# Fused attention, expert layer and MLP on one core: small VectorE steps of the attention stage rewritten, constants loaded later, one copy fewer per key-value half, a new order

## The chip, the cores and the metric

The kernel runs on one core of a Trainium2 chip. The metric is the time of one execution in microseconds (us); lower is better. A core has five engines with their own instruction streams: PE (TensorE, matrix products into PSUM), DVE (VectorE), ACT (ScalarE), POOL (GpSimd) and SP (SyncE, which here issues most of the DMA transfers). SBUF is the working memory, PSUM holds the matrix products in eight banks of 2 KB per partition. An engine works its own instructions off in the order in which they were written; semaphores hold an instruction until what it needs is done.

## The reference

Three stages, one after the other:

```python
q_s, k_s = (q * scale, k * scale)              # q, k, v: 4 batches, 8 heads, 576 tokens, 64 wide
def phi(x):                                    # omega: 128 features x 64
    h = einsum('bhsd,md->bhsm', x, omega) - sum(x * x, -1, keepdims=True) / 2
    return exp(h - max(h, -1, keepdims=True)) / sqrt(m)
q_p, k_p = (phi(q_s), phi(k_s))
kv = einsum('bhsm,bhsd->bhmd', k_p, v); z = sum(k_p, axis=2)
num = einsum('bhsm,bhmd->bhsd', q_p, kv)
den = einsum('bhsm,bhm->bhs', q_p, z)[..., None] + 1e-06
x = num / den                                  # as 2304 tokens x 512
# expert layer: each token goes to the expert with the largest logit (8 experts)
logits = x @ w_gate; expert_idx = argmax(logits, 1); probs = softmax(logits)
out[mask_e] = probs[e] * (maximum(xe @ w1[e], 0.0) @ w2[e])
# MLP: h = out @ w_in (512 -> 2048); g = h, 0 or (h + 1)**2 / 4; result g @ w_out
```

## The kernel before

The attention stage, where nearly the whole change lies, works in units. A unit is half of a block of q or k: four pairs of heads for 256 tokens (two tokens per partition), or a small block that holds the last 64 tokens of two batches. There are 36 units. In each, PE turns the data (`turn`, L640, four 128x128 products with the identity), ACT copies the result out of PSUM (`copy`, L645), PE projects it on omega into two PSUM banks (`project`, L652), DVE takes the row maxima of each bank (`top`, L657), forms the bias of the exponential from maximum and norm (`bias`, L663 and L664), and ACT takes the exponential, four instructions a bank (`exps`, L668). The norms come from the raw block: ACT (for k) or POOL (for q) squares it, POOL adds halves twice (`tree`, L603), and DVE sums the last 16 columns (`total`, L615), once for each of 20 blocks.

When all key units of half the heads of a batch are there, `kv_tasks` sums keys times values over five blocks (L694). ACT copies the result twice: once (`copy1`, L698, tile kvc) as input of a transpose on PE (`turn`, L706), once (`copy2`, L701) into kvz, where the queries read it. The transposed copy goes through the gate's weights (`gates`, L714), so that numerator, denominator and eight logits per head come from one product. There are 8 such halves. `c_tasks` (18 tiles of 128 tokens) turns the query features (L752), multiplies them with kvz (L769), copies the result out (L772, tile nx), and then runs small DVE steps: denominator (`den`), reciprocal (`rec`), logits times reciprocal (`logits`, L785, tile lg), sum over the heads.

`r_tasks` (9 pairs of tiles) is the routing: largest logit (`top`, L825), differences (`shift`, L828, tile rd), a one-hot row (`first`, `first2`, `hot`, L832 to L838, tile ohall), a running count of tokens per expert (`run`, L841, tile rsb), the softmax gate (`gate1` to `gate3`, L852 to L859), the rank of each token in its expert (`count` on PE, `mine`, `mine2`, L884 to L893), and a one-hot row of 384 columns by that rank (`one_b`, L905, tile ob), which PE turns into the list of tokens per expert. POOL scales the output rows (L869, tile xr) and SP stores them. After the last routing a fixed table is worked out on DVE, POOL gathers the first rows, and the expert layer starts with L1215. From there PE is kept full to the end.

The order is not written by hand. `Plan.add` collects tasks with an engine, a cost in ns, a rank, what they come after, and the buffers that they take and use; `Plan.run` picks one task after the other, the earliest start first and among near ones the lowest rank, and gives out buffers from rings, among them the eight PSUM banks (ring "ps"). A bank is given back when its last user is through. The table `NUDGES` holds one number for each task, which shifts its rank.

Of the kernel before, what the change touches and what calls it, by code (L numbers as in the profile page):

```python
# [8 lines left out]
F32 = mybir.dt.float32  # L9
# [27 lines left out]
C_ID, C_TRI, C_IOTA, C_C8, C_WS, C_THR, C_TOK, C_END = 0, 128, 256, 640, 648, 656, 672, 708  # L37
# [172 lines left out]
def kernel(  # L210
# [29 lines left out]
    cs = cp.tile([P, C_END], F32, name="cs")  # L240
    nc.sync.dma_start(out=cs[:, 0:P], in_=consts[:, 0:P])
    ident = cs[:, C_ID:C_ID + P]
# [4 lines left out]
    rsb = cp.tile([P, NTILE + 1, E], BF16, name="rsb")  # L247
    nc.vector.memset(rsb[:, 0, :], 0.0)
    ohall = cp.tile([P, NTILE, E], BF16, name="ohall")
# [229 lines left out]
    with ExitStack() as actx:  # L479
# [4 lines left out]
        def ring(n, shape, name, dtype=F32, pool=ac):  # L484
# [11 lines left out]
            "kvc": ring(1, [P, 4, HD], "kvc"),  # L496
# [43 lines left out]
        def omega_tasks():  # L540
            pb = buf("ps")

            def load():
                for i in range(2):
                    nc.sync.dma_start(out=om2[:, i * HD:(i + 1) * HD], in_=omega)
                nc.sync.dma_start(out=cs[:, P:C_END], in_=consts[:, P:C_END])
# [1195 lines left out]
```

## Time and profile before

| | |
|---|---|
| median of three runs | 783.35 us (782.76 to 785.56) |
| the profiled execution | 784.22 us, of which the span of the instructions is 782.4 us |
| busy share of the span | PE 95%, DVE 67%, ACT 56%, POOL 48% |
| busy time 0 to 20 us | PE 11.72 us, ACT 11.15 us, DVE 7.50 us |
| busy time 180 to 200 us | PE 20.00 us |

The shares over the whole span say little about the attention stage, which fills the first 157 us or so: there four engines are busy at once, and the windows tell which is the fullest. "Busy" counts an instruction from its start to its end, and instructions of one engine overlap at their ends, so that a full PE row is not a PE at its peak. In the rows below an idle time in square brackets names what ended it.

### The profile page before, as it was taken

To read this page: it belongs to the slowest core of one execution; us is meant where nothing else is said; L and a number is where in the kernel's file an instruction comes from. 1 tells how busy PE (TensorE), PEld (TensorE's weight loads), DVE (VectorE), ACT (ScalarE), POOL (GpSimd) and SP (SyncE) were. 2 spreads that over 40 slices of the span, in tenths; PEclk is the share of its full clock that TensorE was granted. 3 is DMA by queue.
4 is the path that set the end of the run, shared out by engine and by line. 5 is a ranking of instruction groups with operands and counts; after the bars stand their busy time and mean duration, and the time that the engine had idled before them with its cause. 6 is when DMAs were issued, how large, how long until landed. Compare 5 with 4: busy or idle time off the path is not lost. (4 is left out here: it accounts for less than half of the span.)

```text
span 782.4 us, 16983 instructions
## 1 busy us (share of the span) xinstructions
PE 746.1 (95%) x6428; PEld 684.1 (87%) x6428; DVE 525.3 (67%) x1075; ACT 439.0 (56%) x1069; POOL 377.5 (48%) x429
## 2 busy tenths in 40 slices
PE   5889999689999999999999999899999999999997
PEld 4778889569999999999998878788998899889985
DVE  3669998964875675665576776776556756575553
ACT  5999989633422222222367766676567665763341
POOL 4738673555556645533737776323343143333212
PEclk9999999899999999999999999999999999999999
DMA  9978411246556766555546778897697986977822
GB/s 221 212 166 230 146 57 30 98 137 202 178 193 196 227 195 197 181 186 162 157 127 261 274 275 289 293 377 221 205 368 174 340 297 162 349 214 299 314 104 85
DMA packets 94236, 164.25 MB, mean 210 GB/s; under 512 B 28528, under 2 KB 61424, under 8 KB 94144
## 3 DMA queue, kind: packets, MB, share of 16 engines
q1 hardware_dynamic: 79680, 94.96, 38.5%
q0 software_dynamic: 14112, 67.44, 26.7%
q8 instruction: 53, 0.87, 0.5%
q10 hardware_dynamic: 352, 0.66, 0.3%
q14 instruction: 39, 0.32, 0.1%
HBM read 122.93 MB, written 40.11 MB: 208 GB/s over the span
## 5 line engine op out<-in xcount | busy, mean ns | idle before, releaser
L1418 PE MATMUL po<-wh,g 128*128 128x512 f32 x288 | 113.9, 395 | 0.9 <-ACT st L1424 0.9
L1420 PE MATMUL po<-wh,g 128*128 128x512 f32 x288 | 113.8, 395 | 0.0
L1419 PE MATMUL po<-wl,g 128*128 128x512 f32 x288 | 113.6, 394 | 0.0
L349 POOL TENSOR_TENSOR wl<-wz,wh 128x256 fp32r<-128x256 f32 (+1 forms) x43 | 40.4, 946 | 96.7 <-ACT wh L363 92.7
L668 ACT ACTIVATE pp<-ps,bi 128x128 f32<-128x128 f32 x288 | 85.5, 487 | 2.6 <-DVE bi L664 2.6
L327 POOL TENSOR_SCALAR wh<-wra 128x1024 fp32r<-128x1024 f32 x43 | 52.1, 1215 | 56.0 <-DMA wra<-in_moe_w_dram 39.3
L1233 PE MATMUL py<-hh,wh 128*128 128x288 f32 (+6 forms) x256 | 77.5, 303 | 0.0
L1215 PE MATMUL ph<-xh,wh 128*128 128x288 f32 (+6 forms) x256 | 76.6, 299 | 0.5 <-ACT xh L1174 0.4
L1216 PE MATMUL ph<-xl,wh 128*128 128x288 f32 (+6 forms) x256 | 76.6, 299 | 0.1
L1217 PE MATMUL ph<-xh,wl 128*128 128x288 f32 (+6 forms) x256 | 76.5, 299 | 0.0
L1235 PE MATMUL py<-hh,wl 128*128 128x288 f32 (+6 forms) x256 | 76.4, 299 | 0.0
L1234 PE MATMUL py<-hl,wh 128*128 128x288 f32 (+6 forms) x256 | 76.3, 298 | 0.0
L1380 DVE TENSOR_TENSOR g<-cl,g 128x384 fp32r<-128x384 f32 x78 | 47.0, 603 | 38.9 <-ACT g L1376 37.9
L1220 ACT ACTIVATE hh<-ph 128x288 fp32r<-128x288 f32 (+6 forms) x64 | 26.8, 418 | 70.0 <-PE ph L1217 67.5
L1420 PEld LDWEIGHTS po<-wh,g 128*128 128x128 f32 x288 | 54.2, 188 | 13.1 <-DVE g L1380 0.4
L1418 PEld LDWEIGHTS po<-wh,g 128*128 128x128 f32 x288 | 54.2, 188 | 12.9 <-ACT st L1424 1.6
L1419 PEld LDWEIGHTS po<-wl,g 128*128 128x128 f32 x288 | 54.3, 188 | 11.4
L1376 ACT ACTIVATE g<-cl 128x384 fp32r<-128x384 f32 x78 | 40.6, 520 | 40.4 <-DVE cl L1375 39.2
L1221 DVE SCALAR_TENSOR_TENSOR hl<-ph,hh 128x288 fp32r<-128x288 f32 (+6 forms) x64 | 29.3, 462 | 48.9 <-ACT hh L1220 48.8
L439 DVE TENSOR_TENSOR wl<-wra,wh 128x1024 fp32r<-128x1024 f32 x43 | 58.9, 1371 | 4.7 <-POOL wh L327 4.7
L657 DVE TENSOR_REDUCE nsq<-ps 128x4 f32<-128x512 f32 x72 | 47.4, 684 | 18.4 <-PE ps L652 18.2
L1238 ACT ACTIVATE yT<-py 128x288 f32<-128x288 f32 (+7 forms) x32 | 13.4, 418 | 82.5 <-PE py L1235 79.6
(223 smaller groups left out, 2166.5 us busy)
## 6 DMA issues: line engine op xcount, KB each, us to landing
yS<-yd POOLq DMA_DIRECT2D x32, 768.0 KB, 12.7
wra<-in_moe_w_dram SPq DMA_DIRECT2D x43, 512.0 KB, 4.2
ys<-yd POOLq DMA_DIRECT2D x25, 768.0 KB, 12.4
wraw<-in_moe_w_dram SPq DMA_DIRECT2D x20, 512.0 KB, 3.9
yd<-tt SPq DMA_DIRECT2D x24, 384.0 KB, 2.4
yd<-ys SPq DMA_DIRECT2D x9, 768.0 KB, 5.2
wra<-in_moe_w_in_dram SPq DMA_DIRECT2D x12, 512.0 KB, 5.5
wra<-in_moe_w_out_dram SPq DMA_DIRECT2D x11, 512.0 KB, 7.2
```

Of the source, the lines that this page charges most:

```text
L327: nc.gpsimd.tensor_scalar(out=hi, in0=t, scalar1=1.0, scalar2=1.0, op0=ALU.mult, op1=ALU.mult)
L439: nc.vector.tensor_sub(lo, t, hi.bitcast(F32))
L668: act.activation(at(ppb)[:, 2 * j + i, :], at(pjb[i])[:, j, :], AF.Exp, bias=r["bi"][:, j, i:i + 1])
L1215: nc.tensor.matmul(ph, lhsT=wh[:, d, c], rhs=xh, start=(d == 0), stop=False)
L1216: nc.tensor.matmul(ph, lhsT=wh[:, d, c], rhs=xl, start=False, stop=False)
L1217: nc.tensor.matmul(ph, lhsT=wl[:, d, c], rhs=xh, start=False, stop=(d == 3))
L1233: nc.tensor.matmul(py, lhsT=wh[:, a, c], rhs=hh, start=(f == 0), stop=False)
L1234: nc.tensor.matmul(py, lhsT=wh[:, a, c], rhs=hl, start=False, stop=False)
L1235: nc.tensor.matmul(py, lhsT=wl[:, a, c], rhs=hh, start=False, stop=(f == 7))
L1418: nc.tensor.matmul(po, lhsT=gh[:, c], rhs=wh, start=(f == 0), stop=False)
L1419: nc.tensor.matmul(po, lhsT=gh[:, c], rhs=wl, start=False, stop=False)
L1420: nc.tensor.matmul(po, lhsT=gl[:, c], rhs=wh, start=False, stop=(f == 3))
```

## The change

1. **Two SBUF inputs avoided.** The result of `rec` is written into the PSUM bank of the second numerator, the small tiles mx, d, mm and ga of the routing into the bank that the rank's count uses. So logits, shift, first, hot and gate2 read one operand from PSUM and one from SBUF. The running count becomes a sum over a tile `seen` that holds counts and one-hot rows side by side. `mine2` sums a second time, into PSUM, and `one_b` compares with that, by a tensor_tensor in place of a tensor_scalar. In the last pair d and mm alone lie in PSUM.
2. **Bias in one sum.** The maximum is taken negated, `total` writes half the bias twice (a second, small sum), and one sum over three numbers per row gives the bias, separately for each of the two banks. The exponential of the first bank no longer waits for the second maximum.
3. **Constants.** The identity has a tile of its own; the other constants (580 columns) are loaded by a task of rank 0 instead of together with omega.
4. **Key-value copy.** `copy1` and its tile are gone. `turn` takes kvz as the stationary operand of four real products with the identity, in place of two transposes.
5. **Costs and order.** A few costs in the plan are changed, buffers are taken earlier, and `NUDGES` is a new table.

```diff
 NUDGES = (
-    -8, 0, 25, -32, -23, 7, 39, 44, 36, -21, 30, 41, 44, -2, -37, -10, 2, 21, 43, -6, 4, -11, 31, -1, -16, -8, 19,
...
+    2, -4, -40, -16, 43, -44, 37, -6, 17, -2, -26, 9, -18, 36, -44, -2, -29, -37, 32, -32, -8, -18, 33, 26, -23,
...
             def load():
                 for i in range(2):
                     nc.sync.dma_start(out=om2[:, i * HD:(i + 1) * HD], in_=omega)
-                nc.sync.dma_start(out=cs[:, P:C_END], in_=consts[:, P:C_END])
+
+            def load_cs():
+                nc.sync.dma_start(out=cs, in_=consts[:, 0:C_ID])
...
-            x = add("SP", 1300, load, -7.5)
-            add("DVE", 130, tri, 1, after=[x])
+            x = add("SP", 1300, load_cs, 0)
+            add("DVE", 130, tri, 8, after=[x])
+            x = add("SP", 100, load, -7.5)
...
             def total():
-                dve.reduce_sum(norms()[:, 0:n, 0], at(sb)[:, 0:n, 0:16], axis=AX, negate=True)
+                m = norms()[:, 0:n]
+                dve.reduce_sum(m[:, :, 0], at(sb)[:, 0:n, 0:16], axis=AX, negate=True)
+                dve.reduce_sum(m[:, :, 1], m[:, :, 0:1], axis=AX, negate=True)
...
-            def bias():
-                r["bi"] = ap.tile([P, 4, 2], F32, name="bi", tag="bi", bufs=6)
-                m = o["norms"]()[:, 8 * hf:8 * hf + 8, :]
-                dve.reduce_sum(m[:, :, 2], m[:, :, 0:2], axis=AX, negate=True)
-                dve.reduce_sum(r["bi"].rearrange("p j i -> p (j i)"), m[:, :, 0:3:2], axis=AX)
+                dve.reduce_max(m[:, i, :], at(pjb[i]), axis=AX, negate=True)
+
+            def bias(i):
...
+                m = o["norms"]()[:, 8 * hf:8 * hf + 8, :].rearrange("p (j i) x -> p i j x", i=2)
+                dve.reduce_sum(r["bi"][:, :, i], m[:, i], axis=AX)
...
-            def copy1():
-                act.activation(at(kcb), at(kvb)[:, :, 0:HD], AF.Copy)
-
...
             def turn():
                 for c in range(2):
-                    nc.tensor.transpose(at(p1)[:, c, :],
-                                        at(kcb)[:, 2 * c:2 * c + 2, :].rearrange("p h d -> p (h d)"), ident)
+                    for i, w in enumerate(HALVES):
+                        nc.tensor.matmul(at(p1)[w, c, :], lhsT=kz[:, 4 * hf + 2 * c + i, 0:HD], rhs=ident,
+                                         start=True, stop=True)
...
-                    r["rden"] = ap.tile([P, H, 1], F32, name="rden", tag="rden", bufs=2)
+                    r["rden"] = at(nmb[1])[:, 0, 96:96 + H].rearrange("p (h o) -> p h o", o=1)
...
+            inner = ("d", "mm") if last else ("mx", "d", "mm", "ga")
...
             def run(j):
-                dve.tensor_add(rsb[:, t0 + j + 1, :], rsb[:, t0 + j, :], oh[:, j, :])
+                with nc.allow_low_precision("counts of at most 18"):
+                    dve.reduce_sum(rsb[:, t0 + j + 1, :], seen[:, t0 + j].rearrange("p i e -> p e i"), axis=AX)
...
             def mine2():
                 dve.reduce_sum(rk, r["pr"], axis=AX)
+                dve.reduce_sum(at(pb)[:, 2, 0:n], r["pr"], axis=AX)
...
-                dve.tensor_scalar(out=r["ob", j], in0=cs[:, C_IOTA:C_IOTA + NB * P], scalar1=rk[:, j:j + 1],
-                                  scalar2=None, op0=ALU.is_equal)
+                dve.tensor_tensor(out=r["ob", j], in0=cs[:, C_IOTA:C_IOTA + NB * P],
+                                  in1=at(pb)[:, 2, j:j + 1].to_broadcast([P, NB * P]), op=ALU.is_equal)
...
-            m = x = add("DVE", 85, top, fast if last else rank, after=[c["end"] for c in cs_])
+            m = x = add("DVE", 85, top, fast if last else rank, after=[c["end"] for c in cs_], take=[pb], use=[pb])
```

How the order moves, at three places. In each name the number behind the underscore is the buffer.

The start on SP, the engine that issues the loads (cs are the constants, om is omega, blk the blocks of q and k), before:

```order
L241 DMA cs<-in_consts_dram 128x128
L590 DMA blk_142<-in_k_dram 128x8x128
L545 DMA om_206<-in_omega_dram 128x64 x2
L546 DMA cs<-in_consts_dram 128x580
L586 DMA blk_143<-in_k_dram 64x8x64 x2
L590 DMA blk_144<-in_k_dram 128x8x128
L590 DMA blk_145<-in_k_dram 128x8x128
L590 DMA blk_146<-in_q_dram 128x8x128
L590 DMA blk_147<-in_k_dram 128x8x128
```

and after:

```order
L244 DMA ident<-in_consts_dram 128x128
L594 DMA blk_142<-in_k_dram 128x8x128
L546 DMA om_205<-in_omega_dram 128x64 x2
L590 DMA blk_143<-in_k_dram 64x8x64 x2
L594 DMA blk_144<-in_k_dram 128x8x128
L594 DMA blk_145<-in_k_dram 128x8x128
L594 DMA blk_146<-in_q_dram 128x8x128
L549 DMA cs<-in_consts_dram 128x580
L594 DMA blk_147<-in_q_dram 128x8x128
```

The 580 columns of constants go from the fourth place to behind the fourth block; the blocks before them keep their order.

The first key-value halves on ACT (kvc and kvz are the two copies, kvt the transposed one, pp the exponentials, th the turned units), before:

```order
L701 ACTIVATE kvz_185<-ps_138 128x4x65
L668 ACTIVATE pp_161<-ps_139,bi 128x128 x4
L698 ACTIVATE kvc_178<-ps_134 128x256
L701 ACTIVATE kvz_185<-ps_134 128x4x65
L645 ACTIVATE th_151<-ps_136 128x512
L668 ACTIVATE pp_160<-ps_135,bi 128x128 x4
L710 ACTIVATE kvt_179<-ps_139 128x256
L698 ACTIVATE kvc_178<-ps_138 128x256
```

and after:

```order
L703 ACTIVATE kvz_184<-ps_134 128x4x65
L674 ACTIVATE pp_162<-ps_136,bi 128x128 x4
L703 ACTIVATE kvz_184<-ps_140 128x4x65
L713 ACTIVATE kvt_178<-ps_137 128x256
L674 ACTIVATE pp_161<-ps_138,bi 128x128 x4
L758 ACTIVATE qt_166<-ps_139 128x512
L758 ACTIVATE qt_167<-ps_136 128x512
L674 ACTIVATE pp_163<-ps_135,bi 128x128 x4
```

The two kvc copies are gone, and the first turned queries (qt) stand among the exponentials here.

The last routing on DVE (the tiles are those named above; blk are the last two output tiles), before:

```order
L905 TENSOR_SCALAR ob<-cs,rank 128x384
L855 SCALAR_TENSOR_TENSOR dall<-rga,dall 128x16
L893 TENSOR_REDUCE rank<-rpr 128x2
L835 TENSOR_REDUCE rmm<-req 128x2
L859 RECIPROCAL dall<-dall 128x16
L838 TENSOR_TENSOR ohall<-req,rmm 128x16
L869 TENSOR_TENSOR blk_143<-nx_173,dall 128x512
L841 TENSOR_TENSOR rsb<-rsb,ohall 128x8
L905 TENSOR_SCALAR ob<-cs,rank 128x384
L869 TENSOR_TENSOR blk_146<-nx_170,dall 128x256
L841 TENSOR_TENSOR rsb<-rsb,ohall 128x8
```

and after:

```order
L867 SCALAR_TENSOR_TENSOR dall<-rga,dall 128x16
L846 TENSOR_REDUCE ps_134<-req 128x2
L901 TENSOR_TENSOR rpr<-ps_138,seen 128x16
L871 RECIPROCAL dall<-dall 128x16
L849 TENSOR_TENSOR seen<-req,ps_134 128x2x8
L905 TENSOR_REDUCE rank<-rpr 128x2
L906 TENSOR_REDUCE ps_138<-rpr 128x2
L881 TENSOR_TENSOR blk_148<-nx_172,dall 128x512
L853 TENSOR_REDUCE seen<-seen 128x8
L918 TENSOR_TENSOR ob<-cs,ps_138 128x384
L853 TENSOR_REDUCE seen<-seen 128x8
L881 TENSOR_TENSOR blk_142<-nx_174,dall 128x256
```

The second sum (ps<-rpr) is new in the chain, one-hot row and count read no second SBUF operand, and gate and scaling of the last tiles stay as they were.

## Rows read from the trace of the kernel before

**Rows 1.** Busy time by stretch; us of the stretch, then each engine (instructions)

```profile
14.00:60.00 46.00, 39.84 (x924) 34.89 (x923) 29.21 (x82) 44.24 (x142) 25.05 (x25) 1.00 0.87 189
60.00:110.00 50.00, 46.13 (x959) 40.65 (x960) 48.02 (x156) 45.81 (x151) 37.79 (x48) 0.97 0.58 167
110.00:140.00 30.00, 30.00 (x708) 27.91 (x705) 26.19 (x97) 29.45 (x102) 13.73 (x24) 1.00 0.08 23
147.00:157.00 10.00, 2.97 (x60) 2.30 (x60) 9.32 (x54) 2.79 (x11) 6.49 (x15) 0.61 0.44 155
```

**Rows 2.** Waits of ACT, 14 to 147 us; total us, times, longest

```profile
ACT pp L668 <- DVE bi L664: 2.1, 4, 0.7
```

**Rows 3.** Groups of DVE by shape, 60 to 110 us; busy us, mean ns, idle before

```profile
L905 DVE TENSOR_SCALAR ob<-cs,rank 128x384 bf16<-128x384 f32 x6 | 4.0, 691 | 0.0
L841 DVE TENSOR_TENSOR rsb<-rsb,ohall 128x8 bf16<-128x8 bf16 x8 | 3.5, 443 | 0.0
L785 DVE TENSOR_TENSOR lg<-nx,rden 128x64 f32<-128x64 f32 x6 | 3.2, 544 | 0.0
L838 DVE TENSOR_TENSOR ohall<-req,rmm 128x16 bf16<-128x16 f32 x4 | 2.3, 566 | 0.0
```

**Rows 4.** The same lines over 0 to 160 us; duration in ns, min/median/max

```profile
L905 DVE TENSOR_SCALAR ob<-cs,rank x18: 365/416/1470, 64.6 to 155.3; 128x384 bf16<-128x384 f32 x18
L841 DVE TENSOR_TENSOR rsb<-rsb,ohall x18: 145/157/1884, 63.4 to 154.2; 128x8 bf16<-128x8 bf16 x18
L785 DVE TENSOR_TENSOR lg<-nx,rden x18: 213/224/1124, 56.4 to 149.4; 128x64 f32<-128x64 f32 x18
L838 DVE TENSOR_TENSOR ohall<-req,rmm x9: 121/174/1011, 62.2 to 152.1; 128x16 bf16<-128x16 f32 x9
```

**Rows 5.** Timeline about 94 to 100 us; start us, duration us

```profile
93.94 1.89 POOL L598 TENSOR_TENSOR sqt<-blk 128x1024 f32<-128x1024 f32 x1
93.97 1.88 DVE L841 TENSOR_TENSOR rsb<-rsb,ohall 128x8 bf16<-128x8 bf16 x1
...
96.19 0.16 DVE L663 TENSOR_REDUCE nsq<-nsq 128x8 f32<-128x16 f32 x1
96.39 0.17 DVE L664 TENSOR_REDUCE bi<-nsq 128x8 f32<-128x16 f32 x1
...
99.48 0.40 ACT L698 ACTIVATE kvc<-ps 128x256 f32<-128x256 f32 x1
99.74 1.17 ACT L668 ACTIVATE pp<-ps,bi 128x128 f32<-128x128 f32 x4
```

**Rows 6.** Groups of DVE by shape, 147 to 166 us

```profile
L869 DVE TENSOR_TENSOR blk<-nx,dall 128x512 f32<-128x512 f32 x1 | 0.7, 679 | 0.0
...
L889 DVE TENSOR_TENSOR rpr<-ps,ohall 128x16 f32<-128x16 f32 x3 | 0.4, 148 | 0.0
...
L869 DVE TENSOR_TENSOR blk<-nx,dall 128x256 f32<-128x256 f32 x1 | 0.4, 414 | 0.0
```

**Rows 7.** Timeline of PE alone, 126 to 136 us

```profile
129.71 2.04 PE L652 MATMUL ps<-oms,th 64*64 64x128 f32 x64
...
133.65 0.42 PE L706 MATMUL ps<-cs,kvc 128*128 128x128 f32 x2
```

**Rows 8.** Timeline of the start

```profile
2.73 0.43 SPq L546 DMA_DIRECT2D cs<-in_consts_dram  x1
...
9.04 0.63 ACT L596 ACTIVATE sqt<-blk 128x512 f32<-128x512 f32 x1 [1.80 <-DMA blk<-in_k_dram]
```

**Rows 9.** Timeline of the last routings, from 135.86 us

```profile
135.86 0.16 DVE L825 TENSOR_REDUCE rmx<-lall 128x2 f32<-128x16 f32 x1
...
144.04 0.42 DVE L905 TENSOR_SCALAR ob<-cs,rank 128x384 bf16<-128x384 f32 x1
...
146.37 1.00 DVE L841 TENSOR_TENSOR rsb<-rsb,ohall 128x8 bf16<-128x8 bf16 x1
...
152.12 0.76 DVE L838 TENSOR_TENSOR ohall<-req,rmm 128x16 bf16<-128x16 f32 x1
```

More of the change, by code (lines that the diff above doesn't have):

```diff
@@ L35 @@
 SQ = -1.0 / 16.0
-C_ID, C_TRI, C_IOTA, C_C8, C_WS, C_THR, C_TOK, C_END = 0, 128, 256, 640, 648, 656, 672, 708
+C_TRI, C_IOTA, C_C8, C_WS, C_THR, C_TOK, C_ID, C_END = 0, 128, 512, 520, 528, 544, 580, 708
 NUDGES = (
[40 rows of a table removed]
[42 rows of a table added]
 )
@@ L237 @@
     yd = [[dram.tile([P, 4 * G], F32, name=f"yd{p}{i}") for i in range(7)] for p in range(NT // G // 2)]
-    cs = cp.tile([P, C_END], F32, name="cs")
-    nc.sync.dma_start(out=cs[:, 0:P], in_=consts[:, 0:P])
-    ident = cs[:, C_ID:C_ID + P]
+    cs = cp.tile([P, C_ID], F32, name="cs")
+    ident = cp.tile([P, P], F32, name="ident")
+    nc.sync.dma_start(out=ident, in_=consts[:, C_ID:C_END])
     trib = cp.tile([P, P], BF16, name="trib")
@@ L246 @@
     lall = cp.tile([P, NTILE, E], F32, name="lall")
-    rsb = cp.tile([P, NTILE + 1, E], BF16, name="rsb")
+    seen = cp.tile([P, NTILE + 1, 2, E], BF16, name="seen")
+    rsb, ohall = seen[:, :, 0], seen[:, 0:NTILE, 1]
     nc.vector.memset(rsb[:, 0, :], 0.0)
-    ohall = cp.tile([P, NTILE, E], BF16, name="ohall")
     rank_ = cp.tile([P, NTILE], F32, name="rank")
@@ L495 @@
             "xr": ring(3, [P, H, HD], "xr"),
-            "kvc": ring(1, [P, 4, HD], "kvc"),
             "kvt": ring(1, [P, 2, P], "kvt"),
@@ L626, in block_tasks @@
                         use=[o["buf"]])
-            t = add("POOL", 50 + 2400 * f, tree, rank - 0.4, after=[t], use=[sb])
-            o["sq"] = add("DVE", 100 + 260 * f, total, rank - 0.3, after=[t], use=[sb])
+            t = add("POOL", 2250 * f, tree, rank - 0.4, after=[t], use=[sb])
+            o["sq"] = add("DVE", 360 if small else 460, total, rank - 0.3, after=[t], use=[sb])
             return o
@@ L655, in top @@
             def top(i):
[L656 to L664 removed]
+                m = o["norms"]()[:, 8 * hf:8 * hf + 8, 2].rearrange("p (j i) -> p i j", i=2)
+                dve.reduce_max(m[:, i, :], at(pjb[i]), axis=AX, negate=True)
+            def bias(i):
+                if "bi" not in r:
+                    r["bi"] = ap.tile([P, 4, 2], F32, name="bi", tag="bi", bufs=6)
+                m = o["norms"]()[:, 8 * hf:8 * hf + 8, :].rearrange("p (j i) x -> p i j x", i=2)
+                dve.reduce_sum(r["bi"][:, :, i], m[:, i], axis=AX)
             def exps(i):
@@ L675, in unit_tasks @@
                         take=[] if c else pjb, use=[thb] + pjb, mode="quarters")
-            ends, tb, t = [], x, x
+            ends, tb, tp = [], x, x
             for i in range(2):
-                t = add("DVE", 600, lambda i=i: top(i), rank + 4.5, after=[t], use=[pjb[i]])
-            t = add("DVE", 290, bias, rank + 1, after=[t, o["sq"]])
-            for i in range(2):
+                tb = add("DVE", 600, lambda i=i: top(i), rank + 4.5, after=[tb], use=[pjb[i]])
+                t = add("DVE", 100, lambda i=i: bias(i), rank + 1, after=[tb, o["sq"]])
                 ends.append(add("ACT", 1003, lambda i=i: exps(i), rank + 2, after=[t] + ends[0:1],
                                 take=[ppb] if i == 0 else [], use=[pjb[i]]))
-            return {"done": ends, "buf": ppb, "ta": ta, "tb": tb}
+            return {"done": ends, "buf": ppb, "ta": ta, "tb": tp}
         def kv_tasks(b, hf, a, st, rank, vload):
             kz = kvz[b][:, 0:H * HZ].rearrange("p (h c) -> p h c", c=HZ)
-            kvb, kcb, ktb, p1, p2 = [buf(n) for n in ("ps", "kvc", "kvt", "ps", "ps")]
+            kvb, ktb, p1, p2 = [buf(n) for n in ("ps", "kvt", "ps", "ps")]
             def head(h):
@@ L729, in kv_tasks @@
                 heads.append(t)
-            c1 = add("ACT", 265, copy1, rank + 1, after=[t], take=[kcb], use=[kvb])
             c2 = add("ACT", 270, copy2, rank + 1, after=[t], use=[kvb])
-            t = add("PE", 216, turn, rank + 1.2, after=[c1], take=[p1], use=[kcb], mode="whole")
+            t = add("PE", 450, turn, rank + 1.2, after=[c2], take=[p1], mode="halves")
             t = add("ACT", 265, copy3, rank + 1.2, after=[t], take=[ktb], use=[p1])
@@ L803, in c_tasks @@
                         use=[nmb[hf]])
-            for fn, cost in ((den, 98), (rec, 113), (logits, 290), (logits_sum, 190)):
-                x = add("DVE", cost, fn, rank - (20 if t >= NTILE - 2 else 3.4), after=[x])
+            for fn, cost in ((den, 98), (rec, 113), (logits, 150), (logits_sum, 190)):
+                x = add("DVE", cost, fn, rank - (20 if t >= NTILE - 2 else 3.4), after=[x],
+                        use=[nmb[1]] if fn in (rec, logits) else [])
             r["end"] = x
@@ L822, in top @@
             def top():
+                o = 0
                 for name, shape in shapes.items():
-                    r[name] = ap.tile(shape, F32, name="r" + name, tag="r" + name, bufs=5)
+                    if name in inner:
+                        c = shape[1] * shape[2]
+                        r[name] = at(pb)[:, 1, o:o + c].rearrange("p (n e) -> p n e", n=n)
+                        o += c
+                    else:
+                        r[name] = ap.tile(shape, F32, name="r" + name, tag="r" + name, bufs=5)
                 dve.reduce_max(r["mx"][:, :, 0], L, axis=AX, negate=True)
@@ L883, in count @@
                 o = at(pb)[:, 0, 0:n * E]
-                nc.tensor.matmul(o, lhsT=oneb, rhs=rsb[:, t0:t0 + n, :].rearrange("p n e -> p (n e)"),
+                nc.tensor.matmul(o, lhsT=oneb, rhs=rsb[:, t0:t0 + n, :],
                                  start=True, stop=False)
-                nc.tensor.matmul(o, lhsT=trib, rhs=oh.rearrange("p n e -> p (n e)"), start=False, stop=True)
+                nc.tensor.matmul(o, lhsT=trib, rhs=oh, start=False, stop=True)
             def mine():
@@ L929, in r_tasks @@
             fast = rank - 20
-            m = x = add("DVE", 85, top, fast if last else rank, after=[c["end"] for c in cs_])
-            x = add("DVE", 85, shift, rank, after=[x])
-            e = add("ACT", 600 if last else 110, expo, fast if last else rank, after=[m if last else x])
+            m = x = add("DVE", 85, top, fast if last else rank, after=[c["end"] for c in cs_], take=[pb], use=[pb])
+            x = add("DVE", 85, shift, rank, after=[x], use=[pb])
+            e = add("ACT", 600 if last else 110, expo, fast if last else rank, after=[m if last else x],
+                    use=[] if last else [pb])
             for fn in (first, first2, hot):
-                x = add("DVE", 90, fn, rank + 0.1, after=[x])
+                x = add("DVE", 90, fn, rank + 0.1, after=[x], use=[pb])
             o = x
@@ L947, in r_tasks @@
             else:
-                e = add("DVE", 90, gate1, rank + 0.2, after=[e])
+                e = add("DVE", 90, gate1, rank + 0.2, after=[e], use=[pb])
                 for j in range(n):
@@ L951, in r_tasks @@
                     for fn in (gate2, gate3):
-                        g = add("DVE", 100, lambda j=j, fn=fn: fn(j, j + 1), rank + 0.2, after=[g])
-                    g = add("POOL", 1180, lambda j=j: scale(j, pool), rank + 0.2, after=[g], take=[xb[j]],
+                        g = add("DVE", 100, lambda j=j, fn=fn: fn(j, j + 1), rank + 0.2, after=[g],
+                                use=[pb] if fn is gate2 else [])
+                    g = add("POOL", 1060, lambda j=j: scale(j, pool), rank + 0.2, after=[g], take=[xb[j]],
                             use=[cs_[j]["buf"]])
                     add("SP", 730, lambda j=j: store(j), rank - 4, after=[g], use=[xb[j]])
-            x = add("PE", 60, count, rank + 0.3, after=[rs], take=[pb], mode="whole")
+            x = add("PE", 60, count, rank + 0.3, after=[rs], use=[pb], mode="whole")
             x = add("DVE", 95, mine, rank + 2.3, after=[x], use=[pb])
-            x = add("DVE", 85, mine2, rank + 0.3, after=[x])
+            x = add("DVE", 180, mine2, rank + 0.3, after=[x], use=[pb])
             ws = []
             for j in range(n):
-                ws.append(add("POOL", 640, lambda j=j: one_a(j), rank + 0.2, after=[o]))
-                ws.append(add("DVE", 550, lambda j=j: one_b(j), rank + 0.4, after=[x, places[-1]]))
+                ws.append(add("POOL", 540, lambda j=j: one_a(j), rank + 0.2, after=[o]))
+                ws.append(add("DVE", 430, lambda j=j: one_b(j), rank + 0.4, after=[x, places[-1]], use=[pb]))
             x = add("PE", 160 * n, place, rank + 0.5, after=ws, take=[p2], mode="whole")
@@ L1032 @@
                 x = add("POOL", 1050, lambda key=key: w_split(key), s + 1, after=[x], use=[wb])
-                add("DVE", 1700, w_flush, s + 1.5, after=[x], use=[wb])
+                add("DVE", 1250, w_flush, s + 1.5, after=[x], use=[wb])
             if s in (33, 35):
```

2 lines of the change are left out of this document (removed), and 80 rows, old and new, of the table NUDGES.

## The prediction

> **What bounds the kernel now.** I read the windows first. From 180 us on PE is busy without a gap (20.00 of 20 us, in the table above), so the later stages keep their length, and what the attention stage gains or loses should arrive at the end unchanged. Inside the attention stage the fullest engine changes [rows 1]: ACT from 14 to 60 us (44.24 of 46), DVE from 60 to 110 us (48.02 of 50, while ACT idles 4.2 us and PE 3.9 us), PE and ACT together from 110 to 140 us (30.00 and 29.45 of 30), and DVE alone from 147 to 157 us (9.32 of 10), when the last routings run and PE has little left. So one microsecond taken from an engine is worth something only in its own stretch.
>
> Next the groups of DVE by shape: why is DVE full from 60 to 110 us? Four small operations have means far above their medians [rows 3, 4]: the product for the logits 544 against 224 ns, the running count 443 against 157, the one-hot row 566 against 174, the comparison of 384 columns 691 against 416. The timeline shows what the long ones are [rows 5]: a running count over eight columns starts at 93.97 us, just after a POOL square began at 93.94, takes 1.88 us and ends with it. All of them read one or two SBUF operands in a form that can meet POOL's, and the long ones look as if they stood until POOL was through. Then the waits: ACT's exponentials waited 2.1 us for the bias in all [rows 2]; that is the visible part of DVE's lateness.
>
> **The change part by part.** *VectorE without two SBUF inputs.* From 60 to 110 us the excess over the median is 6 x 320 = 1.9 us for the logits, 8 x 286 = 2.3 for the count, 4 x 392 = 1.6 for the one-hot row and 6 x 275 = 1.7 for the comparison, 7.5 us together [rows 3, 4]. The change gives all four a form with one SBUF operand (or a sum over one tile), so I let all of it go. If it stays, the edit is worth nothing. What it adds in the same stretch: each comparison becomes a product of 384 elements with a PSUM operand. The two scalings of 256 and 512 columns took 414 and 679 ns [rows 6], which puts 384 at 547, 131 ns above the median now: 6 x 0.13 = 0.8 us. The second rank sum, 4 x 0.16 us by the similar small sum [rows 5] = 0.6 us. The second norm sum depends on the first, and two such dependent sums start 0.20 us apart (96.19 and 96.39) [rows 5]: 6 blocks in the stretch, 1.2 us. The biases are two small sums a unit as before. Net: 7.5 - 2.6 = 4.9 us less DVE in these 50 us.
>
> The price of a PSUM operand is the doubtful item. The one small operation that already reads PSUM and SBUF, 16 elements for the rank, takes 148 ns [rows 6]; the SBUF-only ones of similar length have medians of 157 and 174 [rows 4]. I take nothing for it. [...]
>
> What is 4.9 us of DVE worth there? DVE would fall to 43.1 us of work, under ACT's 45.8 and PE's 46.1, so ACT is next late; the stretch can shorten by at most what ACT idles, 4.2 us [rows 1]. Nothing is the other end. I take 3.0: most of ACT's idle time, because it is DVE's lateness that hands out biases and buffers late, less some that belongs to PE (its order between the modes).
>
> *One copy fewer on ACT.* In the stream of ACT a kvc copy occupies 0.26 us, from its start at 99.48 to the next exponential's at 99.74 [rows 5] (its own 0.40 us runs into that). Eight halves: 2.1 us, in stretches where ACT is among the fullest, so I count all of it; zero is the other end, if PE or DVE sets the pace.
>
> *The transposes that become products.* Two transposes on PE took 0.42 us at 133.65 [rows 7]. The new step is four products of 128 columns, two at a time side by side. For products of 128 columns the projection gives a price: 64 records, two per product and four products at a time, took 2.04 us, so each set that runs at once costs 0.26 [rows 7]. Two sets are 0.51 us, and with the start of the pipe perhaps 0.65. Extra 0.1 to 0.25 us for each half, 0.8 to 2.0 us in all. From 110 to 140 us PE is full [rows 1]; earlier it idles. I let 0.7 us reach the end. The step now waits for the copy into kvz instead of kvc, one copy either way. Behind it on PE stand turns and heads of other units, which the new order places; they wait if the copy is late, as they did before.
>
> *Constants later.* The 580 columns are 128 x 580 x 4 bytes, 0.30 MB. At the 189 GB/s that the loads get from 14 to 60 us [rows 1] they stand for 1.6 us ahead of the second block; ACT waited 1.80 us for that block until 9.04 us, with the constants issued at 2.73 [rows 8]. SP's other loads keep their order, and the constants now stand ahead of the fifth big block. DVE's cast of the triangle moves behind three blocks' maxima, so it should not wait. PE works on the first unit while the second block lands, so not all of the 1.6 us arrives. Between 0 and 1.6 I take 0.9.
>
> *The tail.* From 147 us DVE is the chain. One count of 1.00 us at 146.37 and one one-hot row of 0.76 us at 152.12 [rows 9] stand 0.84 and 0.59 over their medians [rows 4]: 1.4 us to win. Six comparisons at 0.13 and three second sums at 0.16 give back 0.8 and 0.5, less where they overlap. The scaling and gate of the last pair still read two SBUF tiles. I take 0.3, between -1.0 and 1.4.
>
> Sum: 3.0 + 2.1 - 0.7 + 0.9 + 0.3 = 5.6 us. The profiled execution took 784.22 us (span 782.4), which leaves 778.6 for one like it; it stands 0.87 above the median of 783.35, and the forecast for the median is 777.8 us. The ends added, 0 + 0 - 2.0 + 0 - 1.0 and 4.2 + 2.1 - 0.8 + 1.6 + 1.4, are -3.0 and 8.5 us: 786.4 to 774.9.
>
> **The rivals.** *A: the DVE time is freed, but nothing follows it.* From 110 us PE and ACT are full, and the two have 97% of the planned work in 60 to 110 us too; if the new order meets PE there, DVE's 3.0 us stay in DVE's idle time and ACT's copies count for half. Left: 1.0 - 0.7 + 0.9 + 0.3 = 1.5 us, 781.9. For it: DVE's lateness shows in 2.1 us of ACT's waits and no more [rows 2]. Against it: a late DVE also gives PSUM banks back late, and that shows as the wait of whoever takes them.
>
> *B: PSUM banks become the bound, slower.* The bank of a routing was taken when the count began and is now held from the first maximum to the last comparison. In one routing these stand at 135.86 and 144.46 us (144.04 + 0.42) [rows 9], 8.6 us; nine of them hold 77 us of bank time, and the ring has 8 x 127 = 1016 from 20 to 147 us, 7.6%. The second numerator's bank is held through the logits on top. If PE's next turn or projection waits for a bank whenever that share is missing, the 127 us grow by up to 9.6 us, against the 5.6 won: 787.4 us. It decides from about 6 us of such waits on. Against it: the new order was drawn up with these holds in it, and the exponential of the first bank no longer waits for the second maximum, which frees banks sooner.
>
> *C: the excess isn't POOL's doing, or a PSUM operand costs what SBUF's second did.* Then DVE gains nothing and pays the additions of 2.6 us in its fullest stretch: 0 - 1.3 + 2.1 - 0.7 + 0.9 - 0.5 = 0.5 us, 782.9. The pair in rows 5 that ends together speaks against the first half, the 148 ns against the second.
>
> **How the numbers follow.** My forecast 0.56, A 0.22, B 0.12, C 0.10. About 0.5%, 3.9 us, is what a measurement of this kernel can tell from no change: faster means under 779.4, slower over 787.3. Around the forecast the ends spread so that some 0.10 of its 0.56 falls above 779.4, while a happy case of A adds about 0.10 to faster, because a new order can also gain where I count nothing. Faster 0.56, same 0.33, slower 0.11 (nearly all of B). The range for 8 in 10 goes from 773.0, beyond the 774.9 of the terms since an order drawn up anew can close gaps of PE that I priced at nothing, to 784.5, which takes in A and C and leaves out most of B. The forecast's own range is 774.9 to 780.5.
>
> **What would show it.** Right: the medians and means of logits, count, one-hot row and comparison lie together in the profile after, the comparison at about 0.55 us in all places; DVE under 90% in the 50 us where it had 96%; ACT's waits for the bias under 1 us; eight copies fewer on ACT; the second block's square before 8.5 us; the first product of the expert layer about 5 to 6 us earlier, and the time from there to the end as before. Wrong: small steps with a PSUM operand well over 200 ns; PE's loads waiting for ACT or DVE in many places between 60 and 147 us, with routings in between (B); the same small steps still over a microsecond beside POOL (C); or the time after the expert layer's start changed, which nothing here foresees.

## The result and the profile after

The changed kernel takes 776.71 us (median of 4 runs, 776.47 to 776.98) against 783.06 for the kernel before (4 runs, 781.86 to 785.56): ratio 0.9912, 95% interval 0.9892 to 0.9931, so 6.35 us won. The profiled execution took 776.65 us with a span of 774.9 us, 7.5 less than the span before. The forecast was 777.8 us.

Where the 7.5 us arise is read at three landmarks, ahead of the expert layer. Timeline of the kernel before: the last exponentials, the first copy of the fixed table, the first gather.

```profile
142.23 1.22 ACT L668 ACTIVATE pp<-ps,bi 128x128 f32<-128x128 f32 x4
...
156.60 0.15 DVE L1067 COPY t<-ps 128x8 f32<-128x8 f32 x1
...
158.80 1.18 POOL L1162 DMA_INDIRECT xg<-xd,gidx  x1 [3.86 <-DVE ints L1078]
```

The same three in the timeline after:

```profile
135.74 1.18 ACT L674 ACTIVATE pp<-ps,bi 128x128 f32<-128x128 f32 x4
...
151.11 0.15 DVE L1082 COPY t<-ps 128x8 f32<-128x8 f32 x1
...
151.93 1.18 POOL L1177 DMA_INDIRECT xg<-xd,gidx  x1 [2.92 <-DVE prod L1085]
```

The exponentials end 6.5 us earlier (136.92 against 143.45 us), the table copy comes 5.5 earlier, the gather 6.9. The weight loads of the expert layer's first products, before and then after (min, median and max in ns, then first and last start), say the same for the layer itself.

```profile
L1215 PEld LDWEIGHTS ph<-xh,wh x256: 186/188/192, 166.0 to 370.6; 128*128 128x128 f32 x128
```

```profile
L1230 PEld LDWEIGHTS ph<-xh,wh x256: 186/188/192, 159.1 to 363.9; 128*128 128x128 f32 x128
```

The first starts 6.9 us earlier, where the prediction looked for 5 to 6. From there to the end it is 615.8 us against 616.4. So the gain belongs to the attention stage and later stages carry it through. The stretches after that answer to [rows 1]:

```profile
14.00:60.00 46.00, 40.95 (x947) 35.65 (x945) 34.14 (x110) 44.62 (x145) 31.96 (x35) 0.96 0.83 172
60.00:110.00 50.00, 49.23 (x1118) 44.03 (x1117) 44.59 (x170) 48.83 (x161) 39.09 (x48) 1.00 0.65 179
110.00:140.00 30.00, 29.88 (x641) 27.23 (x641) 25.02 (x106) 28.86 (x98) 6.48 (x13) 1.00 0.13 40
```

From 60 to 110 us DVE, the third figure pair, is no longer the fullest: 44.59 of 50 (89%), and PE (49.23) and ACT (48.83) are. That the stretch does more work shows in ACT's exponentials there, before and then after (busy us, mean ns, idle before):

```profile
L668 ACT ACTIVATE pp<-ps,bi 128x128 f32<-128x128 f32 x103 | 30.8, 452 | 2.1 <-DVE bi L664 2.1
```

```profile
L674 ACT ACTIVATE pp<-ps,bi 128x128 f32<-128x128 f32 x114 | 33.4, 453 | 0.0
```

Eleven more in the same 50 us; at the pace before (50 / 103 = 0.49 us each) that is 5.3 of the 6.5 us. The rest lies ahead of 60 us, by when 112 exponentials are done against 109 (the same view, 0 to 60 us):

```profile
L668 ACT ACTIVATE pp<-ps,bi 128x128 f32<-128x128 f32 x109 | 32.8, 555 | 0.4 <-DVE bi L664 0.4
```

```profile
L674 ACT ACTIVATE pp<-ps,bi 128x128 f32<-128x128 f32 x112 | 31.8, 505 | 0.0
```

ACT's wait for the bias [rows 2] is gone. The four small steps that answer to [rows 4], over 0 to 160 us:

```profile
L918 DVE TENSOR_TENSOR ob<-cs,ps x18: 501/546/555, 56.4 to 149.7; 128x384 bf16<-128x384 f32 x18
L853 DVE TENSOR_REDUCE seen<-seen x18: 121/160/170, 53.1 to 147.9; 128x8 bf16<-128x16 bf16 x18
L787 DVE TENSOR_TENSOR lg<-nx,ps x18: 204/220/231, 51.3 to 143.6; 128x64 f32<-128x64 f32 x18
L849 DVE TENSOR_TENSOR seen<-req,ps x9: 104/170/172, 52.9 to 146.6; 128x16 bf16<-128x16 f32 x9
```

Before, the maxima were 1.0 to 1.9 us; now none stands 15 ns over its median, and the means (544, 160, 217 and 151 ns) lie with the medians. Three rest at their median of before with a PSUM operand or as a sum (160 against 157, 220 against 224, 170 against 174 ns), and the comparison has the forecast 0.55 us.

### The profile page after: what moved, and what is told of

Its sections match the earlier page's. It is cut to its first block, busy times and chain, and to the rows that moved or that the text cites. A ratio compares the mean times of both kernels' runs of the same rounds, so it can differ in the third digit from the quotient of the medians.

```text
span 774.9 us, 17116 instructions
## 1 busy us (share of the span) xinstructions
PE 745.1 (96%) x6476; PEld 684.0 (88%) x6476; DVE 515.7 (67%) x1104; ACT 436.7 (56%) x1061; POOL 376.6 (49%) x429
## 5 line engine op out<-in xcount | busy, mean ns | idle before, releaser
L329 POOL TENSOR_SCALAR wh<-wra 128x1024 fp32r<-128x1024 f32 x43 | 50.2, 1170 | 61.2 <-DMA wra<-in_moe_w_dram 26.9
L441 DVE TENSOR_TENSOR wl<-wra,wh 128x1024 fp32r<-128x1024 f32 x43 | 61.0, 1421 | 2.4 <-POOL wh L329 2.4
```

Of the source, the lines that this page charges most:

```text
L329: nc.gpsimd.tensor_scalar(out=hi, in0=t, scalar1=1.0, scalar2=1.0, op0=ALU.mult, op1=ALU.mult)
L441: nc.vector.tensor_sub(lo, t, hi.bitcast(F32))
```

## The experiments

Twelve kernels ran, in three sets of four, each set beside the kernel before (medians 784.34, 785.45 and 784.02 us), so ratios to it are compared. Runs of one kernel spread by 3 us and more there. The changed kernel, run again as a control in the second set, is the measure for the first two sets; the first set ran on another chip, where the kernel before was 1.1 us faster, so its differences go by ratios first.

**Control.** No edit.

> The changed kernel itself once more, as the point of comparison for the others on this chip. Theory: 776.7 us beside 783.1, a ratio of 0.991 to 0.992. Rival (the gain depends on the execution: the experiments before this one lay further apart from run to run): runs spread over 3 us and a ratio nearer to 0.994.

Measured: 779.25 us, 0.9910 [0.9878, 0.9942]: the first result again. Its profile shows where such a kernel spreads: the expert layer starts at 160.7 us instead of 159.1, and at a lower clock. Windows of the control, then of the result after (clock third from the end):

```profile
160.00:166.00 6.00, 5.25 (x26) 5.04 (x27) 2.01 (x5) 2.31 (x6) 1.90 (x2) 0.72 0.43 125
```

```profile
160.00:166.00 6.00, 6.00 (x48) 6.00 (x47) 3.17 (x6) 2.98 (x6) 2.93 (x3) 1.00 0.40 130
```

In these 6 us the granted clock is 0.72 against 1.00. From the layer's start to the end it takes 617.5 us, 1.7 more than the 615.8 above. I therefore give the layer's start of each profile as well.

| profile | layer starts | from there to the end |
|---|---|---|
| before | 166.0 | 616.4 |
| after | 159.1 | 615.8 |
| control | 160.7 | 617.5 |
| two SBUF inputs | 169.1 | 619.1 |
| comparison only | 161.7 | 617.5 |
| no norms | 156.3 | 615.1 |
| two inputs, no norms | 161.2 | 618.5 |
| second copy | 159.6 | 618.5 |
| constants early | 164.3 | 617.3 |
| tail | 160.8 | 618.8 |

**Small steps back to two SBUF inputs**, in the new order:

```diff
-r["rden"] = at(nmb[1])[:, 0, 96:96 + H]...
+r["rden"] = ap.tile([P, H, 1], F32, ...)
...
-inner = ("d", "mm") if last else ("mx", "d", "mm", "ga")
+inner = ()
...
-dve.reduce_sum(rsb[:, t0 + j + 1, :], seen[:, t0 + j]..., axis=AX)
+dve.tensor_add(rsb[:, t0 + j + 1, :], rsb[:, t0 + j, :], oh[:, j, :])
...
-dve.reduce_sum(at(pb)[:, 2, 0:n], r["pr"], axis=AX)
...
-dve.tensor_tensor(out=r["ob", j], ..., in1=at(pb)[:, 2, j:j + 1]..., op=ALU.is_equal)
+dve.tensor_scalar(out=r["ob", j], ..., scalar1=rk[:, j:j + 1], ..., op0=ALU.is_equal)
```

> The changed kernel in its own order, with the small VectorE steps put back as they were: reciprocal, maxima, differences and gate in SBUF, the running count as an addition of two SBUF tiles, the comparison of 384 columns as a tensor_scalar, no second rank sum. Theory (the steps stood behind POOL's instructions): the logits', count's and one-hot steps show maxima over 1 us again, the excess over their medians is 10 us or more, and about 3 us of the 6.4 won are lost: 779 to 781 us. Rival (the order alone won the time, it leaves the steps room): within 1 us of the changed kernel, under 777.7 us. Rival (a PSUM operand costs as much as the wait did): faster than the changed kernel.

Measured: 790.15 us, 1.0068 [1.0042, 1.0094], 1.6% or some 12 us over the control. The long steps are back; DVE's groups of this kernel, 0 to 160 us:

```profile
L916 DVE TENSOR_SCALAR ob<-cs,rank 128x384 bf16<-128x384 f32 x18 | 11.7, 670 | 0.1
...
L787 DVE TENSOR_TENSOR lg<-nx,rden 128x64 f32<-128x64 f32 x18 | 9.7, 546 | 0.2
...
L852 DVE TENSOR_TENSOR seen<-seen 128x8 bf16<-128x8 bf16 x18 | 4.8, 264 | 0.1
...
L866 DVE SCALAR_TENSOR_TENSOR dall<-rga,dall 128x8 f32<-128x8 f32 x16 | 3.3, 228 | 0.0
```

Over the short times (416, 226, 157 and 155 ns) that is 4.6 + 5.8 + 1.9 + 1.2 = 13.5 us; the comparison's shorter form saves 18 x 0.13 = 2.3 of it. The expectation, built on my term of 3.0, missed: in this order most of the DVE time reaches the end. ACT's waits for DVE, 14 to 147 us, show one way:

```profile
ACT rex L860 <- DVE rd L839: 4.0, 4, 1.6
ACT pp L674 <- DVE bi L670: 1.4, 3, 0.7
```

The first are waits of the routing's exponential for the differences, 0.2 us in the control. The second are waits for biases, of which the control has none. This kernel keeps the new bias (part 2 of the change), so part 2 alone doesn't end them; it was not undone by itself. The same kernel's timeline about 102 us shows one of the long steps:

```profile
101.55 2.88 POOL L602 TENSOR_TENSOR sqt<-blk 128x512 f32<-128x512 f32 x2
...
102.67 1.85 DVE L787 TENSOR_TENSOR lg<-nx,rden 128x64 f32<-128x64 f32 x1
104.40 0.72 POOL L607 TENSOR_TENSOR sqt<-sqt 128x256 f32<-128x256 f32 x1
```

POOL's pair of squares ends at 104.43 us and the product of 64 elements, which takes 0.22 elsewhere, at 104.52. The layer starts 8.4 us later than in the control. It then starts at a lower clock, too:

```profile
166.00:172.00 6.00, 3.67 (x17) 3.00 (x16) 1.55 (x4) 1.32 (x4) 3.26 (x4) 0.73 0.62 202
172.00:178.00 6.00, 6.00 (x35) 6.00 (x35) 2.39 (x4) 2.78 (x6) 1.04 (x1) 0.70 0.02 6
```

So about 8 of the 12 us come ahead of the expert layer, and 1.6 behind its start.

**The same with POOL's work taken away.** Two kernels leave the norms out, once from the changed kernel and once from the one with two SBUF inputs:

```diff
-    act.activation(t, raw, AF.Square, scale=0.25)   # or pool.tensor_mul(t, raw, raw)
...
-    pool.tensor_add(t[:, :, 0:w], t[:, :, 0:w], t[:, :, w:2 * w])
...
-    dve.reduce_sum(m[:, :, 0], at(sb)[:, 0:n, 0:16], axis=AX, negate=True)
-    dve.reduce_sum(m[:, :, 1], m[:, :, 0:1], axis=AX, negate=True)
...
-    dve.reduce_sum(r["bi"][:, :, i], m[:, i], axis=AX)
+    dve.reduce_max(r["bi"][:, :, i], at(pjb[i]), axis=AX, negate=True)
```

> The changed kernel in its own order, without the squares, their sums and the bias sums: the norm cancels in the difference from the row maximum, so the negated maximum alone serves as bias. This takes some 10 us of work from ACT, 17 from DVE and 60 from POOL. Theory (ACT is the fullest engine of the attention stage and an order laid out for the squares leaves gaps): 5 to 8 us faster than the changed kernel, 769 to 772 us. Rival (PE sets the pace from 45 to 140 us): under 3 us faster, over 774 us.

> As the kernel without norms (the norm cancels in the difference), and the small VectorE steps put back to two SBUF inputs. POOL then keeps only the scaling of output rows, the token lists and the weights. Theory (the 13 us that two SBUF inputs cost come from waits behind POOL's squares and sums): the cost falls to under 5 us against the kernel without norms, and the logits' mean falls from 546 towards 300 ns. Rival (two SBUF inputs are slow by themselves, or the additional waits come from the order): the cost stays at 10 us or more.

Measured: 776.73 us, 0.9889 [0.9852, 0.9927], and with two inputs 779.72, 0.9914 [0.9880, 0.9948]. The first missed its expectation: the interval overlaps the control's, so what the norms still cost in the changed kernel isn't resolved. The pair is what matters: the two-input forms cost some 12 us with POOL's norm work and 2.0 (by ratios) to 3.0 (by medians) without, where the two intervals overlap. Single profiles show the fall less clearly: at the layer's start the forms cost 8.4 us with the norms and 4.9 without. But the profile of the first kernel here is the shortest of its six runs (773.29 us), and the two spans lie 8.3 us apart; of runs at the same mean clock of 0.991 to 0.992, 776.77 stands against 773.29 and 773.70. DVE's groups of the two-input kernel without norms, 0 to 160 us, and its window:

```profile
L904 DVE TENSOR_SCALAR ob<-cs,rank 128x384 bf16<-128x384 f32 x18 | 8.7, 504 | 0.1
...
L840 DVE TENSOR_TENSOR seen<-seen 128x8 bf16<-128x8 bf16 x18 | 4.8, 265 | 0.1
L775 DVE TENSOR_TENSOR lg<-nx,rden 128x64 f32<-128x64 f32 x18 | 4.7, 271 | 0.2
```

```profile
60.00:110.00 50.00, 49.43 (x1122) 44.48 (x1120) 40.26 (x123) 47.62 (x159) 13.50 (x21) 1.00 0.65 173
```

POOL has 13.50 us of work in the 50 us, against 36.91 in the two-input kernel with norms. The logits' product falls from 546 to 271 ns and the comparison from 670 to 504. The count keeps 265: three of its 18 are long, and each ends with one of POOL's scalings, which are left. The longest, in the timeline:

```profile
143.39 1.04 POOL L868 TENSOR_TENSOR xr<-nx,dall 128x512 f32<-128x512 f32 x1 [2.32 <-DVE lall L779]
143.51 0.94 DVE L840 TENSOR_TENSOR seen<-seen 128x8 bf16<-128x8 bf16 x1
```

So the first half of rival C, that the excess isn't POOL's doing, falls. That the cost falls with it can have two reasons, which these runs don't separate. The excess is shorter (1.6 + 0.8 + 1.9 + 0.5 = 4.8 us by the same four groups, against 13.5), and DVE has more room for it (40.26 us of work in the 50 us, 44.98 in the control). The logits' product, which reads two SBUF tiles, has a mean of 546 ns with POOL's squares and 271 without. The comparison, which reads one SBUF tile and a scalar, stood too (670 ns with them, 504 without).

**The comparison alone** back to one instruction with a scalar operand, without the second rank sum (the last three changed lines of the first diff):

> The changed kernel in its own order, with only the comparison put back to a tensor_scalar that reads SBUF alone, and without the second rank sum. Theory: the comparison takes 0.42 us alone but waits for POOL, in all 18 x 0.15 us of waits against 18 x 0.13 + 9 x 0.09 us saved: even, within 0.7 us of 776.7 us. Rival (the comparison is the step that matters, since it is the longest): 2 us slower or more, over 778.7 us.

Measured: 780.37 us, 0.9945 [0.9926, 0.9964], 0.35% or some 2.7 us over the control, where the forecast's working had it near even. Its line over the span:

```profile
L917 DVE TENSOR_SCALAR ob<-cs,rank x18: 403/424/2045, 54.6 to 149.9; 128x384 bf16<-128x384 f32 x18
```

A median 122 ns lower, but single comparisons of up to 2.0 us. The intervals overlap, so it is likely, not certain, that the product with the longer median is the better form.

**A second copy on ACT:**

```diff
+    act.activation(kvc, at(kvb)[:, :, 0:HD], AF.Copy)
     act.activation(kz[:, 4 * hf:4 * hf + 4, 0:HV], at(kvb)[:, :, 0:HV], AF.Copy)
```

> The changed kernel in its own order with one more copy of 128x256 on ACT ahead of each copy into kvz; nothing reads it. Theory (ACT is among the fullest engines where these copies stand, and PE's turn waits behind them): 8 x 0.26 = 2.1 us lost, 778.3 to 779.2 us. Rival (PE or DVE sets the pace there, or the order leaves ACT room): under 777.4 us.

Measured: 779.44 us, 0.9928 [0.9905, 0.9951]. By ratios the eight copies cost 0.18%, 1.4 us. The intervals overlap: nothing is an answer, and the forecast's 2.1 us are one too.

**Constants early:**

```diff
                 nc.sync.dma_start(out=om2[:, i * HD:(i + 1) * HD], in_=omega)
+                nc.sync.dma_start(out=cs, in_=consts[:, 0:C_ID])
...
             def load_cs():
-                nc.sync.dma_start(out=cs, in_=consts[:, 0:C_ID])
+                pass
```

> The changed kernel in its own order, with the 580 columns of constants loaded right behind omega again, ahead of the second block. Theory of the prediction: 0.9 us lost, 777.2 to 778.2 us, and the second block's square on ACT starts about 0.9 us later than 8.12. Rival (PE's order in the first unit hides it; ACT's first exponentials came no earlier in the changed kernel than before): the square is later, the time the same within 0.4 us.

Measured: 782.02 us, 0.9963 [0.9946, 0.9980]; this interval lies just clear of the control's. It costs 2.8 us by medians, 4.2 by ratios, and the layer starts 3.6 us later than in the control; the forecast of 777.2 to 778.2 missed. Timeline of this kernel at the second block:

```profile
8.83 0.63 ACT L601 ACTIVATE sqt<-blk 128x512 f32<-128x512 f32 x1 [1.59 <-DMA blk<-in_k_dram]
```

and of the kernel after, with the issue of the constants:

```profile
7.46 2.00 SPq L549 DMA_DIRECT2D cs<-in_consts_dram  x1
...
8.12 0.63 ACT L600 ACTIVATE sqt<-blk 128x512 f32<-128x512 f32 x1 [0.65 <-DMA blk<-in_k_dram]
```

The block itself is only 0.71 us later. By 60 us, though, 104 exponentials are done against 112, and eight of them are 2.3 us of ACT (four in 1.17 us). How 0.7 us of a load become 3 or more in this order I did not find out.

**The tail:** the last routing's maximum also in PSUM, and the rank sum that the comparison reads made first.

```diff
+    dve.reduce_max(r["mx2"][:, :, 0], L, axis=AX, negate=True)
...
-    dve.tensor_add(r["d"], L, r["mx"].to_broadcast([P, n, E]))
+    dve.tensor_add(r["d"], L, r["mx2"].to_broadcast([P, n, E]))
...
+    dve.reduce_sum(at(pb)[:, 2, 0:n], r["pr"], axis=AX)
     dve.reduce_sum(rk, r["pr"], axis=AX)
-    dve.reduce_sum(at(pb)[:, 2, 0:n], r["pr"], axis=AX)
```

> The changed kernel in its own order; in the last routing the maximum is also written to PSUM (one more small reduction), so that the last difference no longer reads two SBUF operands, and in every routing the rank sum that the comparison needs comes first. Theory (DVE alone is the chain of the tail; the last difference took 0.78 us beside a POOL scaling): 0.4 to 0.8 us faster than the changed kernel. Rival (the stores of the last rows are what the expert layer waits for, and they hang on the gate, not on the difference): within 0.3 us.

Measured: 778.37 us, 0.9903 [0.9872, 0.9935]: no difference from the control, though the last difference does fall from 0.78 us to 0.17. The 0.4 to 0.8 us of the forecast are too small for these intervals.

**Code and order apart.** Both kernels without their table (`plan.nudge(NUDGES)` left out), and each with the other's, number by number for the tasks that both have:

```diff
-        plan.nudge(NUDGES)
```

> The changed kernel with the table of rank shifts left out, so that the planner orders by ranks and costs alone. Theory (the rewritten steps win by themselves, whatever the order): against the kernel before without its table, 5 to 12 us faster. Rival (the order has to fit the steps, and without a fitted one they win nothing): within 3 us of it. Either way slower than with its table, 785 to 800 us.

> The kernel before with its table of rank shifts left out: the point of comparison for the changed kernel without its table. Theory: slower than with its table by 5 to 20 us, 790 to 805 us, and 5 to 12 us slower than the changed kernel without its table. Rival: within 3 us of that.

> The changed kernel with the table of the kernel before, each task with the shift of its counterpart (the two bias sums both with that of the old bias, the new load of the constants with none). Theory (the steps win, the order adds to it): between the two kernels, 777 to 783 us. Rival (a table fits only its own task list): slower than the kernel before, over 785 us, about where the kernel without a table is.

> The kernel before with the table of the changed one, each task with the shift of its counterpart (the old copy of 128x256 with none). Theory (the new order leaves the old steps beside POOL's work, as in the experiment that put them back): 786 to 793 us. Rival (the order alone carries the gain): under 782 us.

| | own table | no table | the other's table |
|---|---|---|---|
| old steps | 1 | 1.0108 [1.0063, 1.0153] | 1.0084 [1.0057, 1.0110] |
| new steps | 0.9910 [0.9878, 0.9942] | 1.0054 [1.0029, 1.0079] | 1.0073 [1.0046, 1.0100] |

The 0.9910 is the control's, from the second set. A table fits only its own kernel: the other's is worse than one's own by 0.8 and 1.6%. The changed kernel with the old table took 790.89 us where 777 to 783 was expected, a miss; its rival came true. The order alone doesn't carry the gain either: the old steps with the new table took 792.86 us. Without any table the new code still wins 0.54% (795.28 against 788.57 us, 6.7 by medians); the intervals overlap at their ends, so this is likely and not certain. It is the whole new code, with the copy and the constants, so it doesn't price the freed DVE time alone. The logits' product of old and new steps, both without a table (0 to 165 us):

```profile
L785 DVE TENSOR_TENSOR lg<-nx,rden 128x64 f32<-128x64 f32 x18 | 7.2, 402 | 0.2
```

```profile
L787 DVE TENSOR_TENSOR lg<-nx,ps 128x64 f32<-128x64 f32 x18 | 3.7, 216 | 0.2
```

## Why the prediction was right, and where its terms were off

**The mechanism held.** The four steps' means fell to their medians, DVE is no longer the fullest, ACT waits for no bias, and the gain reaches the end at its size. The four kernels with and without two SBUF inputs and POOL's norm work show that the long steps are POOL's doing (13.5 us of excess in the two-input forms with that work, 4.8 without). How much of their price goes with that work is less sure, as said there.

That the sum of 5.6 us lies within 0.8 us of the 6.35 is in part luck: no term was measured by itself in the old order, and the terms below are only partly borne out. One premise was read too widely. PE isn't busy without a gap from 180 us on: before, it has 96.25 of the 100 us from 400 to 500. That the gain comes through is shown by the 615.8 and 616.4 us.

**DVE from 60 to 110 us, 3.0 us, is borne out where it can be read.** The term took most of ACT's 4.2 us of idle time to be DVE's lateness, but the prediction could show 2.1 us of it, and rival A adds "and no more". What the term left to PE for its order between the modes, 1.2 us, was my estimate, and no run shows it. The reading of ACT's waits was too narrow: in the kernel before, ACT also waited for a copy of DVE's into kvz. ACT's waits for DVE, 60 to 110 us, before (beside the 2.1 of [rows 2]) and then after:

```profile
ACT kvz L701 <- DVE kvz L718: 1.4, 1, 1.4
```

```profile
ACT rex L861 <- DVE ps L846: 0.4, 1, 0.4
```

So 3.5 us fell to 0.4, and ACT's busy time rose by 3.0 us (45.81 to 48.83). The stretch gained more, about 5.3 us by the eleven exponentials. Three copies fewer are 0.8 of it (0.26 us each, ACT's term), and some 1.4 us are left that no run traces to a cause; the new order works there too, and PE rose from 46.13 to 49.23 us. Undone in the new order, the same steps cost some 12 us. That is no measure of what they won: the order was made for short steps, and it loses more with long ones than the old order did. Parts undone one by one sum to more than the whole (12 + 1.4 + 3 us or more against 6.35), so no shares can be read from them, and that holds for each part below.

**A PSUM operand cost nothing that shows here**, as I took it: 220 against 224 ns for the logits and 170 against 174 for the one-hot row. Writing to PSUM cost a little here. Two groups after, 0 to 160 us,

```profile
L784 DVE RECIPROCAL ps<-dall 128x8 f32<-128x8 f32 x18 | 3.6, 204 | 0.3
...
L836 DVE TENSOR_REDUCE ps<-lall 128x2 f32<-128x16 f32 x8 | 1.4, 171 | 0.1
```

had means of 189 and 156 ns before, so 15 ns more, which I hadn't priced.

**The copy, 2.1 us, stays open**: making it again cost 1.4 us by ratios, and both 2.1 and nothing lie within the noise.

**The transposes came at the upper end of their price.** One half's four products, two records each, in the timeline of PE after:

```profile
40.82 0.66 PE L709 MATMUL ps<-ident,kvz 128*64 128x128 f32 x8
```

Six of the eight halves take 0.66 us and two 0.61 or 0.62, against 0.38 to 0.44 before [rows 7]: some 0.25 more for a half, 2.0 in all. My 0.14 us for the start of the pipe, on top of the 0.51 for two sets, was a guess; the runs show the 0.66 and not what its parts are. What reaches the end was not measured.

**Constants, 0.9 us, stay open.** The block's delay is as priced: its square on ACT starts at 8.12 us, before at 9.04 [rows 8]. Undone in the new order the part cost 2.8 to 4.2 us, over the end of 1.6 that I had set by the load's own length. But by 60 us the changed kernel is only three exponentials ahead, about 1.3 us at the pace so far (48.6 us for 109), and that holds four copies fewer as well. So the larger figure is a price in the new order and not what the part won. The later load has a cost too, which the prediction put at nothing. DVE's cast of the triangle took 0.57 us before; after, it meets a POOL square and ends 0.08 us behind it:

```profile
19.29 1.89 POOL L602 TENSOR_TENSOR sqt<-blk 128x1024 f32<-128x1024 f32 x1 [0.78 <-DVE nsq L620]
19.33 1.93 DVE L558 CAST trib<-cs 128x128 bf16<-128x128 f32 x1
```

This cast reads a single SBUF operand, so a long step beside POOL doesn't need two of them.

**The tail, 0.3 us, came out as its sum and not as its parts.** From the last exponential to the expert layer it is 22.2 us against 22.6. But to the table copy it is 1.0 us longer, not shorter: one more tile of query work follows the last exponential in the new order. From there to the gather it is 1.4 us shorter, which I hadn't foreseen and didn't test. Of the long steps here one went and another came: before, the last pair's gate took 0.99 us and its difference 0.12; after, 0.16 and 0.78, each still with two SBUF operands.

**Rival B, banks, was not seen.** PE's weight loads after, 20 to 140 us, wait for ACT in a few places; the waits of projection and turn for exponentials, which give banks back, are these (total us, times, longest):

```profile
PEld ps L658 <- ACT pp L674: 1.6, 3, 1.0
PEld ps L646 <- ACT pp L674: 1.2, 4, 0.6
```

The same two had 1.6 and 1.3 us before, so nothing of the 9.6 us that this rival needed was added.

## What to carry to other kernels

When the mean of a small VectorE step stands at twice its median, look at what GpSimd runs beside it before changing anything else: for steps of 8 to 64 elements, moving one small operand to PSUM, or summing over a joined tile, cost 0 to 15 ns here and took away waits of up to 1.9 us. Price such waits from all that the next engine waits for the late one, not from the largest entry alone (3.5 us here, where 2.1 were counted). Where an order fits one kernel, undoing one part in it can overstate that part, so compare also without the order.

## What the runs showed of the hardware

The 384-column comparison with a scalar operand has the shorter median (424 against 546 ns) and still came out about 2.7 us slower in the whole, likely because single ones stood up to 2.0 us. And part of a kernel's spread lies behind the start of the expert layer: the granted clock from 160 to 166 us was 1.00 in the profile after and 0.72 in the control's, and the rest took 615.8 and 617.5 us. PE had worked 3.99 and 3.75 us of the 10 from 140 us on, and what made the clocks differ stays open.
